# Three loads cut at 13 sixteenths of their partitions, in a fused banded-attention and MoE kernel on one core

## The chip, the cores and the metric

The kernel runs on one core of a Trainium2 chip. A time is the device time of one execution in microseconds. The time before is the median of 8 runs. One execution was also taken by the hardware profiler, and all rows of the profile come from that one.

## The reference

Banded attention over 8 batches and 8 heads, then a two-layer block with a smooth ReLU over all 4608 tokens:

```
scores = q @ k^T / 8, kept where |i - j| <= 32     # q, k, v: (8, 8, 576, 64) f32
attn   = softmax(scores);  o = attn @ v
x      = o as (4608, 512)
h      = x @ w_in                                  # w_in (512, 2048)
g      = h if h >= 1, 0 if h <= -1, else (h + 1)^2 / 4
out    = g @ w_out                                 # w_out (2048, 512), out (4608, 512) f32
```

## The kernel before

All matrix work is in bf16. The inputs lie in HBM as f32, and the loads that GpSimd issues change them to bf16 on the way. Two operands stay in SBUF for the whole run: `w_in` as 128 partitions x 4 x 2048 and `w_out` as 128 x 16 x 512.

**Tiling.** Tokens go in 18 blocks of 256, and one batch of attention is 576 tokens. For each block the hidden layer is computed in 8 pieces of 256 columns. The main loop runs over `a`, which counts these pieces. A step `a` does one `project` (TensorE, L488; L513 in the wide middle part), the activation on ScalarE and VectorE (L532 to L539), then what was put down for this step in the table `ev`: pieces of attention (`scores` L228 and L253, `sums` L294, transposes of q and k on TensorE, L188), and some matmuls of the output layer (`pair` L463 for the first blocks, `unit` L448 afterwards). This order is written out by hand, and every engine works in it.

**Loads.** All loads but the first two of q are issued by GpSimd, one instruction each, in program order:

- k of batch 0, first half, as two loads (`load_half`, L86), and v of batch 0 as four (`load_v`, L107);
- four half loads of `w_in` (`load_w_in`, L111). The contraction of 512 lies on 128 partitions x 4, and a half load fills 64 of the partitions for a range of columns. Both halves of a range are needed before a `project` of it;
- the second half of batch 0's q and k, two loads of 128 partitions each (`load_half`), then the other ten half loads of `w_in`; the last two of them are of 512 columns, the others of 256;
- three loads of `w_out` (L116), q and k of batch 1 (L93), `w_out`, v of batch 1, mask work, `w_out` again, and q, k and v of batch 2 (`load_nat` L99, four instructions, and `load_v`).

In the text "the fourth `w_in` load" is the upper half of columns 256 to 511, and "the last `w_in` load" is the upper half of columns 1536 to 2047.

From batch 3 on, q, k and v are loaded from within the main loop. From batch 2 on, q and k are transposed by a DMA that SyncE issues (`xpose`, L195: first q, then k), on the queue that also carries the output stores. The SBUF buffers of the loaded q and k come free when these transposes have read them, so GpSimd's next loads of q wait for the k transpose before.

**Semaphores of the loads.** GpSimd's loads use eight completion semaphores in turn. Before it issues load number n, GpSimd waits until load number n - 8 has landed. The list of waits of the built program names them, `DMASW0` to `DMASW7`.

**Start.** The list of loads that the change touches is these lines:

```
    cuts = [0, 256, 512, 768, 1024, 1280, 1536, DFF]
    w = [(load_w_in, c0, c1, h) for c0, c1 in zip(cuts, cuts[1:]) for h in range(2)]
    put(w[:4] + [(load_half, 1, t, h) for t in range(2) for h in range(2)] + w[4:])
```

Of the kernel before, what the change touches and what calls it, by code (L numbers as in the profile page):

```python
# [14 lines left out]
def kernel(  # L15
# [19 lines left out]
    nc = tc.nc  # L35
# [32 lines left out]
    w_in = const.tile([128, 4, DFF], BF, name="w_in")  # L68
# [9 lines left out]
    qn, kn, vn = {}, {}, {}  # L78
    HD = (slice(0, 64), slice(64, 128))

    def load_half(half, t, h, eng=None, x=None):

        src, dst, nm = ((q, qn, "qh"), (k, kn, "kh"))[t]
        if (0, half) not in dst:
            dst[0, half] = early.tile([128, 2, S], BF, name=nm, tag=nm, bufs=2) if x is None else x
        (eng or nc.gpsimd).dma_start(out=dst[0, half][:, h], in_=src[0].rearrange(  # L86
            "(h y) (l p j) d -> h l p y (j d)", h=2, l=2, p=32)[h][half])

    def load_rows(b, t):
        src, dst, nm = ((q, qn, "qn"), (k, kn, "kn"))[t]  # L90
# [16 lines left out]
        nc.gpsimd.dma_start(out=vn[b][64 * a:64 * a + 64, :, h], in_=v[b, y:y + 2].rearrange("y s d -> (y s) d")  # L107
                            .rearrange("(c r) d -> r c d", r=64))

    def load_w_in(c0, c1, h):  # L110
        nc.gpsimd.dma_start(out=w_in[64 * h:64 * h + 64, :, c0:c1],  # L111
                            in_=moe_w_in.rearrange("(h y d) f -> h d y f", h=2, d=64)[h][:, :, c0:c1])

    def load_w_out(c, k0, k1):

# [5 lines left out]
    for h in range(2):  # L121
        load_half(0, 0, h, (nc.sync, nc.scalar)[h], q32)
    for h in range(2):
        load_half(0, 1, h)
# [19 lines left out]
    def put(todo):  # L144
        for fn, *x in todo:
            fn(*x)

    cuts = [0, 256, 512, 768, 1024, 1280, 1536, DFF]
    w = [(load_w_in, c0, c1, h) for c0, c1 in zip(cuts, cuts[1:]) for h in range(2)]
    put(w[:4] + [(load_half, 1, t, h) for t in range(2) for h in range(2)] + w[4:])  # L150
    put([(load_w_out, 0, k, k + 4) for k in (0, 4, 8)] + [(load_rows, 1, t) for t in range(2)] + [(load_w_out, 0, 12, 16)])
    put([(load_v, 1, n) for n in range(4)])
    P.tensor_copy(band[HD[1], 0:128], band[HD[1], 64:192])
# [340 lines left out]
    for a in range(NF * NB + 2 * NF):  # L494
        wide = WIDE[0] <= a < WIDE[1]
        eng = None if a < 14 else V
# [9 lines left out]
        if a < NF * NB:  # L506
            if wide:
                n, f = divmod(a - WIDE[0], 2 * NF)
                t = WIDE[0] // NF + 2 * n
# [6 lines left out]
            else:  # L516
                t, f = divmod(a, NF)
# [30 lines left out]
        if a >= 40:  # L548
            n = 3 if a < 72 else 4
# [36 lines left out]
```

## Time and profile before

| | |
|---|---|
| median of 8 runs | 307.46 us (306.89 to 308.71) |
| the profiled execution: its own time | 307.48 us |
| its span in the profile | 305.7 us |
| TensorE clock granted, mean | 0.998 |
| TensorE busy | 297.4 us, 97% of the span |
| TensorE busy, 0 to 13 us and 13 to 26 us | 10.47 us and 11.25 us |
| VectorE, ScalarE, GpSimd busy | 241.3, 190.4 and 77.2 us |
| DMA moved | 35.67 MB |
| `w_in` loads | 12 of 128 KB, 2 of 256 KB, as written to SBUF |
| `qh` loads | 2 of 144 KB |

A row of the timeline reads: start, duration, engine, line, operation, tiles, count, and in brackets the idle time of the engine before it with what ended that. A row of the chain reads: start, duration, what ran or was waited for. The trace also holds the time of each of the 16 increments that a load makes on its semaphore when parts of it have landed; where the text speaks of the first and the last completion of a load, it means these.

### The profile page before, as it was taken

What the parts mean: (1) busy time and instruction counts of PE and PEld (TensorE: products, weight loads), DVE (VectorE), ACT (ScalarE), POOL (GpSimd) and SP (SyncE); (2) the same over time, 40 slices, a digit from 0 to 9 for tenths busy, and PEclk for the clock granted to TensorE, in tenths of its full rate; (3) what the DMA queues carried; (4) which work ended last, traced back from release to release, by engine and by line L of the source; (5) the groups of instructions that cost most, each with busy time, mean ns of one, the idle gap of its engine ahead of it and who ended that gap; (6) DMA issues with size and microseconds to landing.
All of it is one profiled execution on the core that took longest, in us unless ns stands there. A gap on an engine that the chain in (4) does not pass through costs nothing.

```text
span 305.7 us, 7846 instructions
## 1 busy us (share of the span) xinstructions
PE 297.4 (97%) x3324; PEld 174.5 (57%) x3324; DVE 241.3 (79%) x378; ACT 190.4 (62%) x318; POOL 77.2 (25%) x92
## 2 busy tenths in 40 slices
PE   7889999999999999999999999999999999999995
PEld 3568888876666666554445444444445444446544
DVE  3278958879888998999988888988888888788700
ACT  3687796648757767677666766665667644444311
POOL 8896660037009104601900730000000000000000
PEclk9999999999999999999999999999999999999999
DMA  9999999999999997997999996551011000010121
GB/s 151 184 196 201 180 185 177 168 157 164 130 192 111 147 144 118 168 155 115 149 151 178 112 173 70 114 113 36 34 36 38 34 36 35 34 36 34 59 80 69
DMA packets 137171, 35.67 MB, mean 117 GB/s; under 512 B 122160, under 2 KB 132912, under 8 KB 137136
## 3 DMA queue, kind: packets, MB, share of 16 engines
q0 software_dynamic: 102976, 18.06, 79.5%
q1 hardware_dynamic: 34016, 16.81, 26.9%
q8 instruction: 26, 0.43, 0.6%
q10 hardware_dynamic: 144, 0.29, 0.4%
q14 instruction: 9, 0.07, 0.1%
HBM read 36.70 MB, written 9.44 MB: 151 GB/s over the span
## 4 chain that ended last, share of the span: by engine, by line
PE 87%; DMA 8%; POOL 3%; issue 1%; ACT 0%; POOLq 0%; ACTq 0%
PE op L448 35%; PE hp L513 23%; PE hp L488 15%; PE bb L294 5%; PE op L463 5%; DMA w_in<-in_moe_w_in_dram 4%; DMA kT<-kn 4%; PE bb L228 2%; POOL w_in L111 2%; POOL vn L107 1%; PE op L439 1%; PE tp L188 1%; POOL kh L86 0%; PE bb L207 0%; PE bb L253 0%
## 5 line engine op out<-in xcount | busy, mean ns | idle before, releaser
L532 ACT ACTIVATE rr<-hp 128x512 f32<-128x512 f32 x144 | 85.3, 594 | 84.3 <-PE hp L513 49.5
L448 PE MATMUL op<-w_out,gT 128*128 128x512 bf16 x496 | 127.0, 380 | 0.0
L538 DVE TENSOR_TENSOR mx<-hp,rr 128x512 f32<-128x512 f32 x139 | 95.7, 689 | 26.3 <-ACT rr L532 24.5
L539 DVE SCALAR_TENSOR_TENSOR gT<-rr,mx 128x512 bf16<-128x512 f32 x139 | 96.4, 693 | 4.8
L513 PE MATMUL hp<-xT,w_in 128*128 128x512 bf16 x320 | 82.1, 379 | 0.0
L448 PEld LDWEIGHTS <-gT 128*128 128x128 bf16 x496 | 46.0, 98 | 47.6
L488 PE MATMUL hp<-xT,w_in 128*128 128x256 bf16 x512 | 66.3, 273 | 1.4 <-DMA w_in<-in_moe_w_in_dram 0.7
L488 PEld LDWEIGHTS <-w_in 128*128 128x128 bf16 x512 | 49.2, 98 | 16.8 <-issue 1.3
L513 PEld LDWEIGHTS <-w_in 128*128 128x128 bf16 x320 | 31.3, 98 | 37.7
L99 POOL DMA_DIRECT2D qn<-in_q_dram x12 | 14.6, 1223 | 92.5 <-DMA kT<-kn 90.5
L236 ACT ACTIVATE pt<-bb 128x1024 bf16<-128x1024 f32 (+1 forms) x33 | 32.8, 1002 | 5.6 <-PE bb L228 4.2
L107 POOL DMA_DIRECT2D vn<-in_v_dram x32 | 27.8, 902 | 5.3 <-DMA w_out<-in_moe_w_out_dram 3.1
L306 DVE TENSOR_TENSOR xT<-bb,rc 128x512 bf16<-128x512 f32 (+1 forms) x32 | 21.0, 657 | 10.0 <-ACT rc L301 9.1
L452 ACT COPY osb<-op 128x512 f32<-128x512 f32 x31 | 18.0, 581 | 12.5 <-PE op L448 12.1
L301 ACT ACTIVATE rc<-lr 128x512 f32<-128x512 f32 (+2 forms) x40 | 23.5, 587 | 1.3
L300 ACT ACTIVATE lr<-bb 128x512 f32<-128x512 f32 (+2 forms) x40 | 22.0, 551 | 0.3 <-PE bb L294 0.3
L202 DVE TENSOR_TENSOR pt<-pt,mask 128x1024 bf16<-128x1024 bf16 (+1 forms) x33 | 20.3, 614 | 0.7 <-ACT pt L236 0.7
L294 PE MATMUL bb<-pt,ones 64*64 64x256 bf16 (+3 forms) x352 | 19.5, 255 | 0.1
L294 PE MATMUL bb<-pt,vn 64*64 64x128 bf16 (+3 forms) x712 | 18.3, 204 | 0.1
L294 PEld LDWEIGHTS <-ones 64*64 64x64 bf16 x352 | 10.3, 105 | 12.5 <-issue 12.5
L294 PEld LDWEIGHTS <-vn 64*64 64x64 bf16 x712 | 16.7, 107 | 0.3 <-DMA vn<-in_v_dram 0.3
L463 PE MATMUL op<-w_out,gT 128*128 128x256 bf16 x128 | 16.3, 273 | 0.0
(61 smaller groups left out, 136.3 us busy)
## 6 DMA issues: line engine op xcount, KB each, us to landing
out_dram<-osb SPq DMA_DIRECT2D x35, 256.0 KB, 2.4
vn<-in_v_dram POOLq DMA_DIRECT2D x32, 144.0 KB, 11.5
qn<-in_q_dram POOLq DMA_DIRECT2D x12, 288.0 KB, 6.7
kn<-in_k_dram POOLq DMA_DIRECT2D x12, 288.0 KB, 9.6
w_in<-in_moe_w_in_dram POOLq DMA_DIRECT2D x12, 128.0 KB, 5.2
w_out<-in_moe_w_out_dram POOLq DMA_DIRECT2D x4, 256.0 KB, 8.2
w_out<-in_moe_w_out_dram POOLq DMA_DIRECT2D x2, 512.0 KB, 12.1
kh<-in_k_dram POOLq DMA_DIRECT2D x4, 144.0 KB, 5.3
```

The source lines that it names most:

```text
L107: nc.gpsimd.dma_start(out=vn[b][64 * a:64 * a + 64, :, h], in_=v[b, y:y + 2].rearrange("y s d -> (y s) d") .rearrange("(c r) d -> r c d", ...
L236: A.activation(p, ps[:, :, :w * n].rearrange(like, y=m), AF.Exp, scale=D ** -0.5)
L294: nc.tensor.matmul(bb[HD[h], a, o + c0:o + c1], ones[HD[a]] if c is None else vn[b][HD[a], c, h], p(a, h), start=n == 0, stop=True, skip_g ...
L300: A.activation(lr[:, :, :D0], bb[:, :, D0:2 * D0], AF.Ln)
L301: A.activation(rc[:, :, :D0], lr[:, :, :D0], AF.Exp, scale=-1.0)
L448: nc.tensor.matmul(op[tt], gT[:, j, home(tt // 2), 128 * (tt % 2):128 * (tt % 2) + 128], w_out[:, j], start=j == 0, stop=j == 15)
L463: nc.tensor.matmul(o[:, tt], gT[:, j, p, 128 * tt:128 * tt + 128], w_out[:, j, 256 * half:256 * half + 256], start=not done, stop=len(done ...
L488: nc.tensor.matmul(hp[:, j], w_in[:, kk, 256 * f + 128 * j:256 * f + 128 * j + 128], xT[:, kk, r0:r0 + TB], start=first and n == 0, stop=l ...
L513: nc.tensor.matmul(hp.rearrange("p n t -> p (n t)"), w_in[:, kk, 128 * f:128 * f + 128], xT[:, kk, r0:r0 + 2 * TB], start=n == 0, stop=n == 3)
L532: A.activation(rr, hp, AF.Relu, scale=0.5, bias=0.5)
L538: V.tensor_max(mx, hp, rr)
L539: V.scalar_tensor_tensor(g, rr, 1.0, mx, op0=ALU.min, op1=ALU.mult)
```

## The change

Three loads are each issued as two instructions, the first for 13 sixteenths of the partitions and the second for the other 3 sixteenths:

- the fourth `w_in` load: 64 partitions become 52 and 12;
- the first of the two loads of the second half of batch 0's q (`qh`): 128 partitions become 104 and 24;
- the last `w_in` load: 64 partitions become 52 and 12.

The bytes, their places and the order of everything else are the same. GpSimd has three instructions more, and from each cut on, load n waits for another load than before, since the eight semaphores are counted by instruction.

```
-    def load_half(half, t, h, eng=None, x=None):
+    def load_half(half, t, h, eng=None, x=None, parts=(0, 128)):
...
-        (eng or nc.gpsimd).dma_start(out=dst[0, half][:, h], in_=src[0].rearrange(
-            "(h y) (l p j) d -> h l p y (j d)", h=2, l=2, p=32)[h][half])
+        rows = src[0].rearrange("(h y) (l p j) d -> h l p y (j d)", h=2, l=2, p=32)[h][half]
+        for p0, p1 in zip(parts, parts[1:]):
+            (eng or nc.gpsimd).dma_start(out=dst[0, half][p0:p1, h], in_=rows[p0 // 4:p1 // 4])
...
-    def load_w_in(c0, c1, h):
-        nc.gpsimd.dma_start(out=w_in[64 * h:64 * h + 64, :, c0:c1],
-                            in_=moe_w_in.rearrange("(h y d) f -> h d y f", h=2, d=64)[h][:, :, c0:c1])
+    def load_w_in(c0, c1, h, parts=(0, 64)):
+        for d0, d1 in zip(parts, parts[1:]):
+            nc.gpsimd.dma_start(out=w_in[64 * h + d0:64 * h + d1, :, c0:c1],
+                                in_=moe_w_in.rearrange("(h y d) f -> h d y f", h=2, d=64)[h][d0:d1, :, c0:c1])
...
-    put(w[:4] + [(load_half, 1, t, h) for t in range(2) for h in range(2)] + w[4:])
+    for n in (3, len(w) - 1):
+        w[n] += ((0, 52, 64),)
+    put(w[:4] + [(load_half, 1, 0, 0, None, None, (0, 104, 128))] + [(load_half, 1, *x) for x in ((0, 1), (1, 0), (1, 1))] + w[4:])
```

## The prediction

> **What bounds the kernel now.** I read the page's busy shares first, then TensorE's timeline for its waits, the chain, and the timelines of the two engines that issue DMAs. The profiled execution took 307.48 us: a span of 305.7 and 1.78 around it. It stands 0.02 above the median of 307.46, so the sums below are made against 307.48. A difference under 0.3%, that is 0.92 us, can't be told from no change.
>
> ```profile
> PE 297.4 (97%) x3324; PEld 174.5 (57%) x3324; DVE 241.3 (79%) x378; ACT 190.4 (62%) x318; POOL 77.2 (25%) x92
> DMA  9999999999999997997999996551011000010121
> ```
>
> TensorE is busy 97% of the span, and it loses only 8.3 us in all. The DMA engines are at 90% or more in 22 of the first 24 slices of 7.64 us. So a load moves the end only where TensorE waits for it, or where it delays something that TensorE waits for later. TensorE's waits for DMA after the first k load are these:
>
> ```profile
> 16.75 0.69 PE L188 MATMUL tp<-ident,kh 128*64 128x128 bf16 x17 [0.25 <-DMA kh<-in_k_dram]
> 18.16 1.03 PE L488 MATMUL hp<-xT,w_in 128*128 128x256 bf16 x8 [0.71 <-DMA w_in<-in_moe_w_in_dram]
> ...
> 118.14 0.42 PE L228 MATMUL bb<-qT,kT 64*64 64x128 bf16 x16 [0.59 <-DMA kT<-kn]
> ```
>
> At 18.16 it waited for the sixth `w_in` load. At 25.22 the chain of work passes through the last one, whose last completion is at 25.09, though TensorE lost only about 0.15 us there. After 25.22 TensorE does not wait until 118.14. There it stood 0.59 us for batch 4's k transpose, and it never waits for a DMA again. So two paths reach 118.14: TensorE's own, with 0.59 us to spare, and a path of DMAs, which sets the end. The second one is in the timelines of SyncE and GpSimd:
>
> ```profile
> 50.17 6.67 SPq L195 DMA_TRANSPOSE qT<-qn  x1
> 56.94 6.26 SPq L195 DMA_TRANSPOSE kT<-kn  x1
> ...
> 74.32 7.76 SPq L195 DMA_TRANSPOSE qT<-qn  x1
> 82.25 5.70 SPq L195 DMA_TRANSPOSE kT<-kn  x1
> ...
> 100.38 6.47 SPq L195 DMA_TRANSPOSE qT<-qn  x1
> 107.02 6.93 SPq L195 DMA_TRANSPOSE kT<-kn  x1
> ```
>
> ```profile
> 66.14 2.43 POOL L99 DMA_DIRECT2D qn<-in_q_dram  x2 [19.64 <-DMA kT<-kn]
> ...
> 92.06 2.45 POOL L99 DMA_DIRECT2D qn<-in_q_dram  x2 [17.68 <-DMA kT<-kn]
> ```
>
> It is a loop: q's load lands, q is transposed, k is transposed, then GpSimd may load the next q. Each round starts from the landing of q's second load (last completions 50.09, 74.16 and 100.23; the q transposes start 0.08 to 0.16 later). TensorE paces none of these steps. So the round that ends at 118.10 began with the landing of batch 2's q at 50.09, and that stands at the end of a DMA backlog that reaches back to the first loads. **A shift of that landing by d moves the end by d, unless TensorE's own path is later by more than d + 0.59.** Batch 3's transpose (landed about 91.5, used at 91.61) has some 0.1 us to spare, batch 2's 1.4 or more, so a late loop is not absorbed earlier, it is merely seen earlier.
>
> **Why the cuts might matter.** In the steady part, the last completions of the fifth to twelfth `w_in` load are 17.35, 18.02, 18.77, 19.43, 20.09, 20.74, 21.48, 22.14: 0.68 us a load. But the 16 completions of one load are spread: for the fifth `w_in` load from 16.14 to 17.35. The late parts set the landing. The fourth `w_in` load has a straggler: its last two completions are 13.52 and 14.10, and seven early parts have become six. At 11.95 a 16 KB instruction fetch of 0.97 us had run on one DMA engine. A second fetch, at 22.02, does the same to the thirteenth `w_in` load (23.38, then 24.05). The delay is not made up: the last completion stays 0.2 to 0.3 us behind the one before it up to 22.14. So each DMA engine works off its own queue at its own rate. The change touches the loads at the stragglers: if 64 partitions are 4 for each of 16 engines, 52 are 4 for each of 13, and three engines get nothing of the first part.
>
> **The sum, part by part.**
>
> *GpSimd's issues.* Three more, of 0.55 to 0.67 us each by the rows of `w_in` and `qh`: at most 3 x 0.67 = 2.0 us. The fifth `w_in` load was issued at 11.80 and its first part landed at 16.14, so 4.3 us lie between, while an unloaded issue (66.14) shows its first packet 1.9 us later, at 68.06. The backlog thus hides 2.4 us, and I price the issues at 0. Without that cover they would cost 2.0.
>
> *The semaphore turns.* Eight instructions in flight now hold up to three cut ones, so about 1.4 full loads less at the first cuts, 1.0 us less of 5.5. For example, the fifth `w_in` load will wait for the third (12.85) and be issued near 13.1 instead of 11.80. By the 1.9 us above its data can start at 15.0, while the earliest DMA engine comes free for it at about 15.4 and the latest at 16.7. So no engine runs dry: 0. Queued behind the waiting instruction are all later loads, which the same cover holds; after the last cut, v of batch 1 is issued up to about 1 us later, lands with 2 us to spare (40.17, its `sums` from 42.38), and the mask copies are not needed until step 14. Batch 2's loads wait on the same predecessors as before.
>
> *The added share of the other engines.* The remainder has to go somewhere. Twelve partitions on twelve engines are one each, a quarter more. On such an engine that is 0.68 / 4 = 0.17 us for the fourth load, 1.30 / 4 = 0.33 for the last (double width; first completions 22.13, 23.41 and 24.73 are 1.3 apart), and for q 0.72 x 2/8 = 0.18 (24 on 12), or 0.36 if 24 fall on 6. Together 0.68 to 0.87. The end markers of three more instructions add 0.02 each (4-byte packets of 22 ns): 0.06. Upper end: +0.93.
>
> *The relief.* Three engines lose up to 0.68 + 0.72 + 1.30 = 2.7 us. What that brings at 50.09 is bounded by the sixteen completions of batch 2's second q load: they run from 48.18 to 50.09 with a mean of 49.29, so perfect balance would gain 0.80, and no more. Taking three engines away from the late end leaves the fourth latest, 49.72, at a gain of 0.37.
>
> *The choice.* Nothing in the trace names the engine behind a completion. If the three relieved ones were the three latest, the end would move by -0.37 + 0.68 = +0.3. If one late engine is not among them, it moves by +0.7. If the remainder falls on different engines each time, nearer to 0. The latest completions at 50.09 have been through five instruction fetches by then, which hit different engines (the straggler at 24.05 is a new one), so I don't expect the three relieved to be the three latest. I take +0.4, with 0 and +0.93 as ends. TensorE's own path moves by as much at 25.22 (no slack there) and stays inside its 0.59: d decides. Sum: 307.48 + 0.4 = 307.9 us.
>
> **Two rules weighed.** The trace's half loads land 0.68 us apart, so a load in the backlog has no fixed cost that shows. The Trainium skill's page "DMA: Bandwidth & Descriptors", in "Anatomy of one DMA — SWDGE (gpsimd) path", fits about 2.0 us fixed for every DMA, which speaks against cutting; three more would be 6 us if none overlapped, by estimate, and here the rows decide for overlap. The same page, under "Why a DMA increments its semaphore by 16 and not by 1", says a load uses the largest number of engines up to 16 that divides both sides' slowest dimension: 13 for 52 and 104, 12 for 12, 6 for 24, starting at a moving place, with an exception that starts at engine 0. No row of this trace shows a load on fewer than 16.
>
> **The rivals.**
>
> *Balance wins (0.2).* The relieved engines are the late ones, and the remainder lands on early engines with 1 us in hand. For it: the cuts stand at the loads behind the two fetches. Against it: only 3 of 16 engines have room made, and 12 pay. It gives -0.4 to -0.8 at 50.09, and TensorE must come 0.2 earlier at 118 than its slack of 0.59 allows, which the 0.71 at 18.16 can give: 306.9, from 306.7 to 307.1. Past -0.92 it would need a loop that also runs faster. That is possible: the three k transposes took 8.5, 9.2 and 11.1 us to land for the same work, so how they meet other traffic is worth 1 us or more either way.
>
> *The parts run on few engines (0.12), the slower side.* If 52 partitions went to 4 engines, each would carry 13 instead of 4: 9 x 0.17 + 9 x 0.33 for the two `w_in` loads, 4.5 us, and 104 on 8 adds 5 x 0.09 = 0.45. The place is the last `w_in` load at 25.09 and d at 50.09: up to 312.4. It decides once an engine's added work exceeds its lead plus 0.92, some 2 us. No row speaks for it.
>
> *It doesn't reach the end (0.13).* Spare work elsewhere in the backlog hides the cuts: 307.5.
>
> **The numbers.** The forecast, slower by 0 to 0.93, holds 0.55, the rivals 0.2, 0.12 and 0.13. Faster by over 0.92 us: part of the first rival, with a loop that meets its traffic better, 0.11. Slower by over 0.92: the few engines 0.12, and 0.15 for the forecast's upper end with a loop that meets it worse, 0.27. The same: 0.62. The range from 306.7 (full balance) to 309.0 (0.93 and 0.6 of a worse loop) leaves out the few engines and a little of the faster tail.
>
> **What would show it.** Right: the fourth `w_in` load's last completion before 14.10; the spread of later loads no narrower; the q transpose of batch 2 0.4 later than 50.17; the wait at 118.14 still on kT. Wrong: that transpose earlier than 49.8 (balance), a `w_in` wait near 25 us of over 1 us (few engines), GpSimd idle less but DMA share under 9 in slices 2 to 6 (the issues not covered).

## The result, and the profile after

The change made the kernel slower by half a per cent: a median of 309.04 us (307.42 to 310.19, 11 runs; the record lists one more, of 307.88 us, that the median leaves out) against 307.45 us for the kernel before (306.85 to 309.30, 32 runs), a ratio of 1.0051 with a 95% interval of 1.0035 to 1.0066. Forecast were 307.9 us, and the range ended at 309.0. The profiled execution was the fastest of the eleven, 307.42 us, so I read it beside a second one of the same kernel, 309.48 us (span 307.7), which is told below as `e12_change_again`.

Busy times and the DMA row of the first profile hardly differ from before: TensorE has 0.5 us more.

```profile
PE 297.9 (97%) x3324; PEld 174.9 (57%) x3324; DVE 241.5 (79%) x378; ACT 190.6 (62%) x318; POOL 78.7 (26%) x95
...
DMA  9999999999999999995998996550011010010121
```

The waits tell more. Before, the matmuls on the last `w_in` load started like this, with no wait long enough for the view to list:

```profile
25.22 1.91 PE L488 MATMUL hp<-xT,w_in 128*128 128x256 bf16 x16
```

TensorE's timeline in the first profile, idle time in brackets:

```profile
16.64 0.69 PE L192 MATMUL tp<-ident,kh 128*64 128x128 bf16 x17 [0.28 <-DMA kh<-in_k_dram]
18.11 1.03 PE L492 MATMUL hp<-xT,w_in 128*128 128x256 bf16 x8 [0.78 <-DMA w_in<-in_moe_w_in_dram]
25.96 1.91 PE L492 MATMUL hp<-xT,w_in 128*128 128x256 bf16 x16 [1.03 <-DMA w_in<-in_moe_w_in_dram]
```

And in the second profile:

```profile
18.41 1.03 PE L492 MATMUL hp<-xT,w_in 128*128 128x256 bf16 x8 [0.87 <-DMA w_in<-in_moe_w_in_dram]
...
27.29 1.91 PE L492 MATMUL hp<-xT,w_in 128*128 128x256 bf16 x16 [1.58 <-DMA w_in<-in_moe_w_in_dram]
30.64 1.03 PE L467 MATMUL op<-w_out,gT 128*128 128x256 bf16 x8 [0.57 <-DMA w_out<-in_moe_w_out_dram]
```

The matmuls on the last `w_in` load, which started at 25.22 before, start at 25.96 and 27.29. The wait ahead of them was some 0.15 us and is now 1.03 and 1.58 us. The wait at 118.14 for batch 4's k transpose is gone in both. SyncE's transposes in the first profile:

```profile
51.48 6.36 SPq L199 DMA_TRANSPOSE qT<-qn  x1
57.94 6.14 SPq L199 DMA_TRANSPOSE kT<-kn  x1
...
101.04 6.13 SPq L199 DMA_TRANSPOSE qT<-qn  x1
107.33 6.72 SPq L199 DMA_TRANSPOSE kT<-kn  x1
```

Batch 2's q is transposed 1.31 us later than before (50.17), batch 4's k only 0.31 later (107.02). The tile view of `kT` gives 9.4 us from that issue to the landing, and gave 11.1 before. So in this profile the loop of DMAs gave back what it had been handed. In the second profile it did not:

```profile
52.58 6.90 SPq L199 DMA_TRANSPOSE qT<-qn  x1
...
110.15 5.98 SPq L199 DMA_TRANSPOSE kT<-kn  x1
```

There batch 2's q is 2.41 us later and batch 4's k 3.13 later. That k lands after 8.7 us, at 118.83, and TensorE first uses it at 120.19 without a wait, 2.05 us later than the 118.14 of before: TensorE's own path is the later one.

Now the stretch of the `w_in` loads. GpSimd's timeline before, of which the prediction quoted only one time, then in the second profile:

```profile
11.80 1.95 POOL L111 DMA_DIRECT2D w_in<-in_moe_w_in_dram  x3
14.38 4.53 POOL L111 DMA_DIRECT2D w_in<-in_moe_w_in_dram  x7 [0.64 <-DMA w_in<-in_moe_w_in_dram]
```

```profile
13.06 0.63 POOL L113 DMA_DIRECT2D w_in<-in_moe_w_in_dram  x1 [0.16 <-issue]
14.64 6.10 POOL L113 DMA_DIRECT2D w_in<-in_moe_w_in_dram  x10 [0.95 <-DMA w_in<-in_moe_w_in_dram]
```

Before, three loads go out from 11.80 on, and the eighth has to wait. Now one goes out at 13.06, and the sixth has to wait: eight instructions back stands the first part of the fourth load, which landed at 14.36. The sixth load is issued at 14.64 instead of 12.46. What that did to the DMA engines is in the windows from 12 to 24 us (length, busy time of TensorE, weight loads, VectorE, ScalarE and GpSimd with instruction counts, granted clock, DMA share, and last GB/s; the share adds up the packets' times over 16 engines, counts packets that overlap twice, and so passes 1), for before, the first and the second profile:

```profile
12.00:24.00 12.00, 10.47 (x194) 7.33 (x193) 7.58 (x12) 9.49 (x18) 10.39 (x16) 1.00 1.34 197
```

```profile
12.00:24.00 12.00, 10.27 (x196) 7.38 (x195) 7.73 (x12) 9.52 (x17) 11.15 (x18) 1.00 1.32 188
```

```profile
12.00:24.00 12.00, 9.88 (x188) 6.81 (x187) 7.50 (x11) 9.12 (x16) 10.55 (x17) 1.00 1.26 167
```

The DMA engines no longer move what they moved before, 167 GB/s against 197, though the page's slices of tenths still say 9. I call the time from a load's issue to its first completion its **lead**. Before, no load issued between 10 and 20 us has a lead under 3.73 us. In the second profile it falls to 2.56, for the sixth `w_in` load.

### The profile page after: what moved, and what is told of

Same layout as the page of the kernel before. It is cut to its first block, busy times and chain, and to the rows that moved or that the text cites. A ratio compares the mean times of both kernels' runs of the same rounds, so it can differ in the third digit from the quotient of the medians.

```text
span 305.6 us, 7850 instructions
## 1 busy us (share of the span) xinstructions
PE 297.9 (97%) x3324; PEld 174.9 (57%) x3324; DVE 241.5 (79%) x378; ACT 190.6 (62%) x318; POOL 78.7 (26%) x95
## 4 chain that ended last, share of the span: by engine, by line
PE 90%; POOL 5%; DMA 2%; issue 1%; ACT 0%; POOLq 0%; ACTq 0%
PE op L452 36%; PE hp L517 23%; PE hp L492 17%; PE bb L298 6%; PE op L467 5%; POOL w_in L113 3%; DMA w_in<-in_moe_w_in_dram 2%; PE bb L232 2%; PE op L443 1%; POOL vn L108 1%; PE tp L192 1%; POOL kh L88 1%; POOL qh L88 1%; PE bb L211 0%; PE bb L257 0%
## 5 line engine op out<-in xcount | busy, mean ns | idle before, releaser
L298 PEld LDWEIGHTS <-ones 64*64 64x64 bf16 x352 | 10.3, 105 | 12.5 <-issue 12.5
```

What stands on the lines that cost most here:

```text
L298: nc.tensor.matmul(bb[HD[h], a, o + c0:o + c1], ones[HD[a]] if c is None else vn[b][HD[a], c, h], p(a, h), start=n == 0, stop=True, skip_g ...
```

## The experiments

The texts of the expectations name their theories by letters. A: the uneven load of the 16 DMA engines costs. B: the parts start at a DMA engine that moves from one execution to the next. C: three more instructions, each with its turn among the eight. D: the queue of GpSimd's loads runs short; as D1 because of the turns of eight, as D2 because of the time or work that each load instruction takes on its way.

**Is it the uneven cut?** The same three loads cut in the middle, and the change with an 11-partition load (read by nobody) behind all others. The second one aimed at a start place on the DMA engines that might carry over from one execution to the next.

```diff
# e1_half: the change, with
-        w[n] += ((0, 52, 64),)
+        w[n] += ((0, 32, 64),)
-    put(w[:4] + [(load_half, 1, 0, 0, None, None, (0, 104, 128))] + [(load_half, 1, *x) for x in ((0, 1), (1, 0), (1, 1))] + w[4:])
+    put(w[:4] + [(load_half, 1, 0, 0, None, None, (0, 64, 128))] + [(load_half, 1, *x) for x in ((0, 1), (1, 0), (1, 1))] + w[4:])
```

> The same three loads are cut, in the middle: 32 and 32 partitions, 64 and 64. There are as many instructions, and the semaphore turns are the same, as with the change, but both parts divide evenly by 16. Theory A (uneven load: the cut at 13 sixteenths leaves three DMA engines out and gives the other ones more): nothing to be uneven, so 307.4 to 307.8, the time before. Theory C (three more instructions, and other loads waited for in the turns of eight): as slow as the change, 308.7 to 309.3. Theory B (the place at which a load on fewer than 16 DMA engines starts moves on from execution to execution): 307.4 to 307.8 as A, and no difference between the profiled execution and the timed ones.

```diff
# e4_end11: the change, and at its end
+    spare = const.tile([128, 16], BF, name="spare")
+    nc.gpsimd.dma_start(out=spare[0:11], in_=q[0, 0, 0:11, 0:16])
```

> The change, and behind all other loads one load of 11 partitions x 16 numbers that nobody reads. Theory B, by what the Trainium skill's page DMA: Bandwidth & Descriptors says under Why a DMA increments its semaphore by 16 and not by 1: the cuts use 13 + 12 + 13 + 6 + 13 + 12 = 69 engines in turn, five places past a full round of 16; 11 more bring the start back. Theory B without the page: if the place is carried over, any such load changes what the next execution meets, and with this one each execution is like the first, so the timed runs come to 307.4 to 307.9, as the profiled execution of the change did. Theory A: the small load lies late, where DMA is nearly idle, and changes nothing: 308.7 to 309.3.

Measured: the middle cut takes 308.87 us, ratio 1.0044 (1.0029 to 1.0059), the extra load 308.8, ratio 1.0040 (1.0020 to 1.0059). Neither can be told from the change's 1.0051. So the cost does not need uneven shares: what they add is 0.2 us by these medians, give or take 0.7 by the intervals. Theory B falls too, since it expected 307.4 to 307.9 of the extra load. The Trainium skill's page "DMA: Bandwidth & Descriptors", in "Why a DMA increments its semaphore by 16 and not by 1", would by its general rule put 13, 12 and 6 engines on the parts of the change and 16 on the halves. In these runs that made no difference that can be measured (1.0051 against 1.0044).

**Which of the cuts?** Only the last `w_in` load, and only the other two.

```diff
# e2_last_only: the change, with
-    for n in (3, len(w) - 1):
+    for n in (len(w) - 1,):
-    put(w[:4] + [(load_half, 1, 0, 0, None, None, (0, 104, 128))] + [(load_half, 1, *x) for x in ((0, 1), (1, 0), (1, 1))] + w[4:])
+    put(w[:4] + [(load_half, 1, 0, 0, None, None, (0, 128))] + [(load_half, 1, *x) for x in ((0, 1), (1, 0), (1, 1))] + w[4:])
```

> Only the last w_in load is cut, at 52 of 64 partitions. Theory A: TensorE's wait near 25 us is later by about the 0.33 us that a quarter more of 1.30 us costs, and the landing of batch 2's q as well, so 307.7 to 308.2. Theory B: a start that moves by 13 + 12 = 25 places per execution, so timed runs apart from the profiled one by up to 1.5 us. Theory C: a third of the effect, about 308.0.

```diff
# e3_first_two: the change, with
-    for n in (3, len(w) - 1):
+    for n in (3,):
```

> Only the fourth w_in load and the q load are cut, the last w_in load is whole. Theory A: 0.17 + 0.18 us of added share, 307.6 to 308.2, with TensorE's wait near 25 us at most 0.5 longer than before. If e2 and this one together give less than the 1.6 us of the change, the cuts act on each other. Theory C: two thirds of the effect, about 308.5.

Measured: the last alone 307.25 us, ratio 0.9999 (0.9974 to 1.0025); the first two 308.47, ratio 1.0044 (1.0025 to 1.0063). The cost sits at the first two, and theory C's even thirds do not hold (it gave the last alone 308.0). The last stands at the end of the stretch, and only wide loads of about 1.3 us each follow it. (The profiled execution of the last cut alone, 310.06 us, is its slowest of twelve.)

**Data or instruction?** The kernel before with its loads whole and three unread loads of 16 x 16 elements at the places of the cuts; then the same three behind the first three `w_out` loads.

```diff
# e5_tiny3: before, with
+    spare = const.tile([16, 48], BF, name="spare")
+    def tiny(n):
+        nc.gpsimd.dma_start(out=spare[:, 16 * n:16 * n + 16], in_=q[0, n, 0:16, 0:16])
-    put(w[:4] + [(load_half, 1, t, h) for t in range(2) for h in range(2)] + w[4:])
+    put(w[:4] + [(tiny, 0), (load_half, 1, 0, 0), (tiny, 1)] + [(load_half, 1, *x) for x in ((0, 1), (1, 0), (1, 1))] + w[4:] + [(tiny, 2)])
# e6_tiny3_late: before, with the same loads in another place
-    put([(load_w_out, 0, k, k + 4) for k in (0, 4, 8)] + [(load_rows, 1, t) for t in range(2)] + [(load_w_out, 0, 12, 16)])
+    put([(load_w_out, 0, 0, 4), (tiny, 0), (load_w_out, 0, 4, 8), (tiny, 1), (load_w_out, 0, 8, 12), (tiny, 2)])
+    put([(load_rows, 1, t) for t in range(2)] + [(load_w_out, 0, 12, 16)])
```

> The kernel before, with the three loads whole, and three loads of 16 partitions x 16 numbers that nobody reads: behind the fourth w_in load, behind the first q load, and behind the last w_in load. Theory D (the queue runs dry: each load instruction takes some 0.6 us of GpSimd's issue and one of the eight turns whatever its size, and in the stretch of w_in loads the data takes only 0.68 us each, so three instructions that bring no data leave the DMA engines without work between 14 and 24 us): as slow as the cut in the middle, 308.3 to 309.3, and DMA under 180 GB/s somewhere between 14 and 24 us. Theory A (the shares are uneven) and any other that lies in the cut data itself: 307.2 to 307.8, and 193 to 200 GB/s throughout.

> The kernel before and the same three unread loads, but one behind each of the first three loads of w_out, where a load's data takes 1.3 us. Theory D: there the data is longer than the issue, so the queue stays full: 307.2 to 307.9. A cost of each instruction wherever it stands (its end markers, a turn of the semaphores): 308.3 to 309.3.

Measured: 309.05 us, ratio 1.0060 (1.0038 to 1.0081), and late 307.74, ratio 1.0009 (0.9991 to 1.0027). Three loads that move next to nothing cost what the cuts cost, as far as the intervals tell. So the change's cost can come from more load instructions among the short loads, with no data cut. GpSimd's timeline with the three early ones shows the same wait as the change's second profile, ahead of the sixth `w_in` load:

```profile
13.20 0.67 POOL L111 DMA_DIRECT2D w_in<-in_moe_w_in_dram  x1
14.87 5.51 POOL L111 DMA_DIRECT2D w_in<-in_moe_w_in_dram  x9 [1.00 <-DMA w_in<-in_moe_w_in_dram]
```

**GpSimd's time, or the rate at which loads are supplied?** Three fills of 128 x 512 elements in place of the unread loads; and all `w_in` loads cut to the first 128 columns of their range.

```diff
# e9_memset3: before, with
+    spare = const.tile([128, 512], BF, name="spare")
+    def stop():
+        P.memset(spare, 0.0)
+    put(w[:4] + [(stop,), (load_half, 1, 0, 0), (stop,)] + [(load_half, 1, *x) for x in ((0, 1), (1, 0), (1, 1))] + w[4:] + [(stop,)])
# e8_supply: before, with (base(c): the first column of the load that holds column c)
+        nc.gpsimd.dma_start(out=w_in[64 * h:64 * h + 64, :, c0:c0 + 128],
+                            in_=moe_w_in.rearrange("(h y d) f -> h d y f", h=2, d=64)[h][:, :, c0:c0 + 128])
...
+            nc.tensor.matmul(hp[:, j], w_in[:, kk, base(256 * f):base(256 * f) + 128],
...
```

> The kernel before with its loads whole, and three fills of an unread tile of 128 x 512 by GpSimd at the three places of the cuts. They take GpSimd's time as a load instruction does, but no turn of the eight semaphores and no DMA. Theory D1 (what counts is the turns: an instruction without data fills one of eight places in flight): 307.2 to 307.7, as before. Theory D2 (what counts is the time that GpSimd spends, which puts each later load's issue back): 308.3 to 309.3, as with three unread loads.

> The kernel before, with only the first 128 columns of each w_in load brought in (the matmuls of the other columns read these in their place, which leaves out that part of the computation): the same 14 instructions and as many rows each, with half or a quarter of the bytes. The data can then go at 0.34 us a load, and the spacing of the landings shows how fast loads are supplied. Theory D: 0.6 us a load or more, and not 0.34; if it widens to 0.8 or 0.9 from 16 us on, when VectorE is busy, the supply itself slows there. If the landings come 0.35 to 0.45 apart, the supply is not what limits, and theory D falls.

Measured: the fills 307.29 us, ratio 0.9999 (0.9980 to 1.0019). They take 0.54 to 0.63 us each, and the wait for the turn shrinks by what they take earlier: the eighth `w_in` load leaves at 14.39, where it left at 14.38. GpSimd's timeline:

```profile
8.73 0.62 POOL L151 MEMSET spare<- 128x512 bf16 x1
...
9.76 0.63 POOL L151 MEMSET spare<- 128x512 bf16 x1
...
14.39 4.48 POOL L111 DMA_DIRECT2D w_in<-in_moe_w_in_dram  x7 [0.61 <-DMA w_in<-in_moe_w_in_dram]
```

With the narrow loads (one execution, 306.5 us, and its matmuls leave out the columns that are not loaded) GpSimd issues every 0.60 us. From the fifth `w_in` load on the first completions follow 0.37 to 0.55 apart at first and 0.50 to 0.70 from the tenth on, when the lead has shrunk to 2.14 us. So a load instruction does not cost a fixed 0.7 us on its way, and the loads come as fast as they are issued once the lead is used up. That lies between the two outcomes which the expectation named.

**Can fewer instructions pay it back?** The change with two pairs of `w_in` loads joined (columns 1024 to 1535); the change with the first four joined to two; and the kernel before with the first four joined.

```diff
# e7_merge_cut: the change, with
+    cuts = [0, 256, 512, 768, 1024, 1536, DFF]
# e10_merge_first_cut: the change, with
+    cuts = [0, 512, 768, 1024, 1280, 1536, DFF]
-    for n in (3, len(w) - 1):
+    for n in (1, len(w) - 1):
+    put(w[:2] + [(load_half, 1, 0, 0, None, None, (0, 104, 128))] + [(load_half, 1, *x) for x in ((0, 1), (1, 0), (1, 1))] + w[2:])
# e11_merge_first: before, with the same list of cuts and
+    put(w[:2] + [(load_half, 1, t, h) for t in range(2) for h in range(2)] + w[2:])
```

> The change with all three cuts, and two w_in loads fewer: columns 1024 to 1535 come as two loads of 512 columns in place of four of 256. The uneven shares are as in the change, the instructions are one more than before in place of three. Theory D: most of the loss comes back, 307.3 to 308.2, and DMA stays above 180 GB/s from 14 to 24 us; a wait of up to 0.4 us for the wider load near 22 us is the price. Theory A: 308.7 to 309.3.

> The change with all three cuts, and the first four w_in loads (256 columns each) issued as two of 512: one instruction more than before instead of three, and the two saved stand ahead of the stretch that ran dry. Theory D: the lead is kept, DMA above 180 GB/s from 14 to 20 us, 307.2 to 308.2; the first hidden pieces may start up to 0.4 us later, which the waits for k and for the sixth load take up. Anything else that the cuts do by themselves: 308.5 to 309.3.

> The kernel before with the first four w_in loads issued as two of 512 columns and no cut: two instructions fewer than before. Theory D: the queue did not run dry before, or hardly, so there is little to gain: 306.5 to 307.6. If the time falls below 306.5, the kernel before was itself short of lead in most executions.

Measured: joined late 309.86 us, ratio 1.0063 (1.0034 to 1.0091): the expectation missed, in the time and in the rate (178 GB/s from 12 to 24 us). TensorE now waits for the wider load, as its timeline says. That load's last completion is at 24.00, where the same columns were in at 22.14 before; the expectation had allowed a wait of 0.4 us.

```profile
24.14 1.86 PE L492 MATMUL hp<-xT,w_in 128*128 128x256 bf16 x8 [2.31 <-DMA w_in<-in_moe_w_in_dram]
```

Joined early, the change comes to 308.08, ratio 1.0031 (1.0004 to 1.0059), so part may be paid back; its interval overlaps that of the change. Without the cuts the join brings nothing: 307.25, ratio 0.9996 (0.9980 to 1.0013). No version here that computes everything beats the kernel before.

**The change once more**, for a second profile.

> The change once more, for a second profile of it: the first is the fastest of its runs (307.42 us, median 309.04). Theory D with the turns as the cause: w_in loads issued later than before from the fifth on (11.80), DMA between 12 and 24 us under 197 GB/s, and the time made up of what TensorE lost up to the matmuls of the last w_in load (start 25.22 before) less the 0.59 us of the wait for kT, which then no longer occurs: if this run takes 309.0, they start near 27.4; if it takes 307.5 again, near 25.9. Theory A, as the prediction had it: a wait at 118 us for kT that is still there, and longer.

It took 309.48 us beside 307.93 for before, and its last `w_in` matmuls start at 27.29, about as the turns had it; the wait at 118 us that theory A expected is not there. Its rows are above.

**One late landing, or the turn as such?** Two unread loads behind the fourth `w_in` load, or ahead of it. Ahead of it, that load's late landing gates another load than behind it.

```diff
# e13_tiny2_behind: before, with tiny as in e5_tiny3 and
+    put(w[:4] + [(tiny, 0), (tiny, 1)] + [(load_half, 1, t, h) for t in range(2) for h in range(2)] + w[4:])
# e14_tiny2_ahead: before, with tiny as in e5_tiny3 and
+    put(w[:3] + [(tiny, 0), (tiny, 1)] + w[3:4] + [(load_half, 1, t, h) for t in range(2) for h in range(2)] + w[4:])
```

> The kernel before, with two unread loads of 16 x 16 directly behind the fourth w_in load, which often lands late. Theory D1 (the turns of eight: GpSimd stands before the load whose turn the late landing holds, and all later loads go out at 0.60 us each from there): the fourth load now holds the sixth w_in load instead of the eighth, so the eighth is issued some 1.2 us later than 14.38, and the queue runs dry: 308.3 to 309.2, like e3 with as many instructions. Theory D2 (every load instruction puts the supply back by itself, wherever it stands): the same 308.3 to 309.2.

> The same two unread loads, directly ahead of the fourth w_in load. The instructions are as many and the data the same. Theory D1: the fourth load holds the eighth again, as in the kernel before, and the sixth and seventh wait only for the unread loads, so the eighth goes out near 14.4 to 15.0: 307.2 to 307.9. Theory D2: 308.3 to 309.2, as with the two behind it.

Measured: 309.41 us, ratio 1.0082 (1.0054 to 1.0111), and 309.16, ratio 1.0073 (1.0045 to 1.0100). The place makes no difference that can be told, and D1 as it was put there, with one late landing to blame, missed (it expected 307.2 to 307.9 ahead). So it is not one late landing alone. That left two theories: the turn of eight in general, or the work that an added load makes in the queue.

**The turn without any added load.** Six loads get the turn that two added loads would give them, by a copy of one element that the load six back brought; and, as control, the same six copies of an element of the load eight back, for which they wait anyway.

```diff
# e15_turn6: before, with (e16_turn8: n - 8)
+    def peek(n):                      # p, x: one element that load n wrote
...
+        P.tensor_copy(spare[p:p + 1, n % 8:n % 8 + 1], x)
+    late = [(load_half, 1, t, h) for t in range(2) for h in range(2)] + w[4:6]
+    put(w[:4] + [y for n, x in enumerate(late, 10) for y in ((peek, n - 6), x)] + w[6:])
```

> No load is added or cut. Ahead of each of the six loads behind the fourth w_in load (the four half loads of q and k, the fifth and the sixth w_in load) GpSimd copies one element that load n - 6 brought, so that these six wait for load n - 6 and not for load n - 8: just the turns that two added loads give them in the runs with two unread loads. If the turn of eight is what costs (D1: each added load takes a place among the eight in flight), this is slower like those runs: ratio 1.005 to 1.009, the last w_in matmuls between 26.5 and 28 instead of 25.22, and under 180 GB/s between 12 and 24 us. If it is the added load itself (D2: its work in the queue of GpSimd's loads), nothing: 0.998 to 1.002, the last w_in matmuls between 25.1 and 25.6, and 194 to 197 GB/s.

> The same six copies of one element, but from load n - 8, which the load behind the copy waits for in any case. It tells what the copies themselves cost. Both theories expect nothing: 0.998 to 1.002, the last w_in matmuls between 25.1 and 25.6.

Measured: the nearer turn 309.65 us, ratio 1.0084 (1.0054 to 1.0114); the control 307.96, ratio 1.0016 (0.9998 to 1.0033). GpSimd's timeline with the nearer turn, around the fifth and sixth `w_in` load:

```profile
13.89 0.18 POOL L161 COPY spare<-w_in 1x1 bf16<-1x1 bf16 x1 [0.80 <-DMA w_in<-in_moe_w_in_dram]
14.01 0.63 POOL L111 DMA_DIRECT2D w_in<-in_moe_w_in_dram  x1
14.68 0.18 POOL L161 COPY spare<-w_in 1x1 bf16<-1x1 bf16 x1
14.80 5.51 POOL L111 DMA_DIRECT2D w_in<-in_moe_w_in_dram  x9
```

TensorE's timeline and the window of 12 to 24 us of the same kernel:

```profile
27.90 1.91 PE L502 MATMUL hp<-xT,w_in 128*128 128x256 bf16 x16 [1.45 <-DMA w_in<-in_moe_w_in_dram]
```

```profile
12.00:24.00 12.00, 8.92 (x160) 6.28 (x158) 7.37 (x11) 8.57 (x15) 10.39 (x19) 1.00 1.20 159
```

The control's TensorE timeline and window:

```profile
25.31 1.91 PE L502 MATMUL hp<-xT,w_in 128*128 128x256 bf16 x16
...
119.11 0.42 PE L242 MATMUL bb<-qT,kT 64*64 64x128 bf16 x16 [0.84 <-DMA kT<-kn]
```

```profile
12.00:24.00 12.00, 9.89 (x191) 7.04 (x190) 7.49 (x11) 9.10 (x17) 10.79 (x18) 1.00 1.33 194
```

This decides. The nearer turn alone, with every load whole and none added, brings the whole cost of two added loads (1.0084 against 1.0082), and the copies alone bring none that can be told. The turns are enough for the cost, and nothing that can be told is left over for an added load's own work.

The runs side by side. "Ratio" is that of all timed runs; the other columns are from one profiled execution each. "Own" is the time of that execution in us, "last" the start of the matmuls on the last `w_in` load, "lead" the smallest of the loads issued between 10 and 20 us.

| kernel | ratio | own | last | GB/s, 12 to 24 us | lead |
|---|---|---|---|---|---|
| before | 1 | 307.48 | 25.22 | 197 | 3.73 |
| e9, three fills | 0.9999 | 307.49 | 25.50 | 197 | 3.77 |
| e16, control | 1.0016 | 308.43 | 25.31 | 194 | 3.59 |
| e6, three late | 1.0009 | 306.90 | 25.40 | 195 | 3.50 |
| e11, before joined | 0.9996 | 307.20 | 25.15 | 194 | 3.28 |
| e10, change joined | 1.0031 | 307.85 | 26.35 | 186 | 3.25 |
| e7, change joined late | 1.0063 | 309.86 | 28.39 | 178 | 2.97 |
| e3, two cuts | 1.0044 | 308.46 | 26.90 | 172 | 2.90 |
| the change, first profile | 1.0051 | 307.42 | 25.96 | 188 | 2.88 |
| e2, last cut alone | 0.9999 | 310.06 | 27.45 | 184 | 2.78 |
| e1, middle cuts | 1.0044 | 308.92 | 27.42 | 159 | 2.70 |
| e13, two behind | 1.0082 | 308.99 | 26.80 | 170 | 2.69 |
| e14, two ahead | 1.0073 | 309.29 | 27.83 | 168 | 2.69 |
| e15, nearer turn | 1.0084 | 309.40 | 27.90 | 159 | 2.64 |
| e5, three early | 1.0060 | 309.91 | 27.25 | 162 | 2.57 |
| the change, second profile | 1.0051 | 309.48 | 27.29 | 167 | 2.56 |
| e4, change and a last load | 1.0040 | 308.80 | 27.31 | 173 | 2.23 |

Where the lead stays above 3.2 us, the rate is 186 GB/s or more and the execution takes 306.90 to 308.43 us. Where it falls under 3, the rate is 159 to 184 and the execution takes 308.46 to 310.06. One row does not fit: the first profile of the change, with a lead of 2.88 (at a part of the cut q load) but 188 GB/s and 307.42 us. The row of e2 fits its own execution, which is its slowest; its other eleven took 306.48 to 308.54.

**A second cost in three rows.** In the profiled executions of e4, e7 and e14 the granted TensorE clock is one half for 3.41 us, from 19.29, 23.76 and 19.65 on. In e4's windows this reads 0.50:

```profile
20.00:22.00 2.00, 2.00 (x33) 1.21 (x35) 0.34 (x1) 0.60 (x1) 1.90 (x4) 0.50 1.41 190
```

That is why the eight matmuls of e7 above take 1.86 us, where eight take 1.03 to 1.05 elsewhere, and it is part of the late "last" in these rows. These three executions have a mean clock of 0.993. Nine timed runs of e7, e10, e11, e13, e14 and e15 have 0.992 to 0.994, with no trace to show why, and the rest have 0.998 or more. Without the low ones e7's median is 308.50 in place of 309.86, so half of its loss may be this; those of e13 and e15 are 309.36 and 309.40, and the finding on the turns stands. The change itself has no such run. The half clock begins in or after a wait of TensorE in all three, but the wait of 1.58 us in the change's second profile did not bring it, and what does is not shown.

## Why the prediction was wrong

**What was right.** TensorE waits for loads in the first 31 us and hardly anywhere else. The issue of the fifth `w_in` load was expected near 13.1 and came at 12.90 and 13.06. Slower was held likelier than faster, but slower by over 0.92 us, which came (1.59), had only 0.27. The rivals of balance and of few engines do not explain it (e1 costs the same with even parts). Of the signs, batch 2's q transpose came 1.31 and 2.41 later in place of 0.4, and the wait at 118.14 was gone. A DMA share under 9, the sign of issues that are not covered, could not show, since the share is still 1.26 at 167 GB/s. A `w_in` wait of over 1 us near 25 us was named as the sign of few engines, and it came for another reason: a sign that two causes share tells nothing between them.

**The step that failed first: the cover of 2.4 us** in "GpSimd's issues", and with it "no engine runs dry: 0" in "The semaphore turns". Both terms were put at 0; e15 prices nearer turns alone, six loads by two places, at 2.3 us. The 2.4 was 4.3 us from issue to first completion less 1.9 us from issue to first packet. These are two different marks. The like term is the lead of a load that finds the queue empty: 2.56 in the second profile and 2.64 in e15, each the first load after a wait for its turn. So the cover was 4.34 - 2.6 = 1.7 us at the fifth load, and 3.73 - 2.6 = 1.1 at the eighth. Against this stands the delay: the prediction worked it out for the fifth load alone (1.3 us) and took that as the end of it. The sixth is 14.64 - 12.46 = 2.2 us late in the second profile, since its turn is that of the straggling fourth load. 2.2 is more than 1.7, and the queue runs empty. The paragraph's own measure says the same of the sixth load: its data can start at 14.64 + 1.9 = 16.5, while the first completion of the load before it is at 15.98. (The sum of that paragraph was also short. Among the eight instructions before the sixth load stand four parts of two loads, so two loads' data is missing, some 1.4 us, and not 1.4 loads and 1.0 us.)

**Why it is not made up, but grows.** GpSimd issues these loads every 0.60 us, and the DMA engines took 0.68 us for one. Lead once lost comes back by some 0.08 us a load, and nine instructions remain. That says why the loss stays. But by last completions it is 0.26 us at the sixth load (18.28 against 18.02) and 2.07 at the last (27.16 against 25.09), so most of it arises behind the load that found the queue short. The windows from 18 to 24 us, before and in the second profile:

```profile
18.00:24.00 6.00, 5.84 (x137) 4.44 (x138) 4.29 (x8) 5.03 (x10) 5.32 (x8) 1.00 1.36 198
```

```profile
18.00:24.00 6.00, 5.47 (x132) 3.96 (x132) 4.50 (x7) 5.02 (x10) 5.76 (x9) 1.00 1.27 148
```

In slices of 1 us the loads move 147 to 176 GB/s from 16 to 22 us and 113 and 124 in the next two, where before they move 192 to 199, then 193 and 195.

**The second step that failed: "d decides".** The prediction let the loop of DMAs carry a delay to 118.14 unchanged, with TensorE's own path inside its 0.59. But TensorE's path lost 2.80 us (33.26 against 30.46 for the matmuls that follow its last wait for a load). Less the 0.59 this is 2.2, and the execution took 2.00 more than before. In the first profile the same sum gives 0.74 - 0.59 = 0.15, and it took 0.06 less. The loop is not rigid either: the q transpose of batch 2 came 1.31 and 2.41 later in the two profiles, the k transpose of batch 4 landed 1.35 earlier and 0.73 later than before. In the control e16 batch 2's q transpose starts at 50.29, only 0.12 later than before, and batch 4's at 102.36, 1.98 later; there the loop does decide (0.84 us of wait at 119.11), and that profiled execution took 308.43. So both paths must be summed, and the later one counts.

**The terms of uneven shares and of relief** (0.68 to 0.87 and up to -0.80, whence the +0.4) priced something that e1 and e5 do not need and cannot tell from nothing (0.2 us, give or take 0.7). That 309.04 lies so near the range's upper end of 309.0 is luck: it came by another road. The estimate from the Trainium skill's fixed 2.0 us per DMA ("Anatomy of one DMA — SWDGE (gpsimd) path"), 6 us for three, is not what happened either. Three cost about 1.6, and e15 has the cost without an added DMA.

**What stays open.** That the turns start the loss is shown; how it grows is not. The rate stays near 150 GB/s for several microseconds after the lead is back (3.42 to 3.59 for loads issued from 17.04 to 18.25 in the second profile). The engines lack packets then: from 16 to 21 us the DMA share is 1.19 to 1.37 against 1.43 to 1.45 before, while a packet takes about as long (a mean of 58 to 72 ns in the slices against 57 to 62). The DMA engines drift apart then: the eighth to twelfth `w_in` load have 1.36 to 2.29 us between first and last completion, against 1.26 to 1.33 before. Whether that is the cause, or GpSimd supplies the packets more slowly there, wasn't tried. That the first profile got off lightly (0.74 us at the last `w_in` load) goes with an earlier landing of the gating part (13.43 instead of 14.36; its straggler, 14.07, is in the fourth load's second part). What sets this from one execution to the next wasn't tried either, beyond the instruction fetches that the prediction tells of.

## What to carry to other kernels

Where loads take a semaphore in turn, the unit in flight is the instruction, not the byte: a load cut in two, or a tiny load added, shortens the queue of data for the next seven loads. Before cutting loads, compare the issue's delay with the cover, and measure both to the same mark (issue to first completion, once in the full queue and once in an empty one); then ask whether the issuing engine is fast enough to win the lead back (here 0.60 us an issue against 0.68 us a load: it isn't). An added instruction cost nothing that could be told where the loads behind it are long (e2, 0.9999; e6, 1.0009).

## What the runs showed of the hardware that I had not expected

- A queue that had run short did not return to full rate for 8 us: 113 to 176 GB/s of loads, against 192 to 199 in the same stretch before (second profile).
- Three loads of 0.5 KB cost the loads around them as much as the three cuts do (1.0060 against 1.0051), and places among the eight alone cost as much as two such loads (1.0084 against 1.0082).
- Three pieces of GpSimd work of 0.5 to 0.6 us between the loads cost nothing that could be told (0.9999): the wait for the turn shrinks by what they take, and the eighth `w_in` load leaves at 14.39 instead of 14.38.
- The k transpose of batch 4 took 8.7, 9.4 and 11.1 us to land for the same work in the second profile of the change, the first, and before. Of these only the one of 11.1 was waited for; in e16 one of 10.3 was.
- The granted TensorE clock was one half for 3.41 us in single executions (the profiled ones of e4, e7 and e14), from a time at which TensorE had just waited for loads.
